# Two-bank score tiles, unscaled k and an ordered start of attention, in a fused attention and expert kernel

## The chip, the cores and the metric

The kernel runs on one core of a Trainium2 chip. The metric is the device time of one execution in microseconds. A core has TensorE (PE, with its weight loads shown apart as PEld), VectorE (DVE), ScalarE (ACT), GpSimd (POOL) and SyncE (SP), which issues the loads here. Matmul results go to eight banks of PSUM, each of 512 float32 numbers for each partition.

## The reference, cut to what matters

Attention with 2 batches, 8 heads, 576 positions and head size 64 is the sum of two softmax attentions: a banded one, and one over positions averaged in fours, whose result is repeated four times. Its output feeds a gated layer (gate, value and output weights), and that an expert layer with eight experts and a normalised routing.

```python
def sm_attn(qq, kk, vv):
    s = scale * np.matmul(qq, kk.transpose(0, 1, 3, 2))      # scale = 1/8
    s = s - np.max(s, axis=-1, keepdims=True)
    a = np.exp(s)
    a = a / (np.sum(a, axis=-1, keepdims=True) + 1e-09)
    return np.matmul(a, vv)
# q_d, k_d, v_d: means over 4 neighbouring positions
out_up = np.repeat(sm_attn(q_d, k_d, v_d), 4, axis=2)
mask = np.abs(pos[:, None] - pos[None, :]) < 4
...                                                          # banded softmax attention
x = out_up + out_local
h = silu(x @ w_gate) * (x @ w_val) @ w_out
out = sum over 8 experts e of P[:, e] * (relu(h @ w1[e]) @ w2[e])   # P from 8 row and column normalisations
```

## The kernel before, in words

Sixteen heads are worked in eight pairs; the two heads of a pair share one k tile and one q tile, whose halves are zeroed so that each head has its own contraction. The banded attention is cut into five windows of 128 positions. `scores(h)` adds the mask by a matmul with an identity (L397, L402), then the window products (L400, L404) and the pooled products of `qd` and `kd` (L406). VectorE takes the maxima (L409 to L411, in fact minima, because k is scaled by -1/8), ScalarE the seven exponentials with their sums (L415 to L420), VectorE the sum and the reciprocal (L423, L424), GpSimd the normalisation (L426, L428). `turn(h)` transposes the result on TensorE (L437 to L441), and ScalarE copies it back (L443 to L445). `combine(pr)` multiplies by v (L457, L465); ScalarE copies the pooled part (L468), VectorE adds it (L474), and the sum is split into two float16 numbers (L169, L170 in `split`).

`pooled(pr)` scales k in place on ScalarE (L373), sums k and q by fours on VectorE (L374, L381) and scales kd (L375). `pooled_v(pr)` does the same for v on GpSimd (L386 to L390). `bank` gives two single-bank tiles out of six for the scores, the transposes or the outputs of a head or pair. Four heads (`AHEAD`) are started before the first is transposed; then each head's transposition is followed by the start of the head four later.

Between the pairs, gate and value weights, which arrive as float64, are converted for use: `conv_gv(f)` loads 1 MB (L186), rebuilds float32 numbers (L198 to L205) and takes their maximum (L220); `prep_gv(f)` finds a power of two (L139 to L142, across partitions with L160 to L162) and splits the weights. `gv_step(0, f, True)` does three early gate steps (matmuls at L177) during pairs 4, 6 and 7. After attention the rest of the gated layer and the experts follow.

The order of the instructions on each engine is made by a planner from the order in the program, priorities, and the costs that it assumes; `issue_after(ins)`, wrapped as `gate(ins)`, forces what stands inside it behind `ins` on the engine of `ins`, without a wait between engines. All loads are in SP's queue. Semaphores follow from the tiles: a reader in a PSUM bank is kept apart from writers in the same bank of a tile.

## Time and profile before

| | us |
|---|---|
| median of 3 runs | 1045.02 |
| lowest and highest run | 1041.98, 1045.06 |
| span of the profiled execution | 1041.1 |
| PE busy | 1013.4 |
| DVE busy | 756.6 |
| ACT busy | 457.7 |
| POOL busy | 81.3 |

The span runs from the first to the last instruction; for the profiled execution the page gives its span alone, and the time of a run also takes in what lies before and after it. Busy time of PE is the time in which a matmul is in work, also a slow one. Attention fills about the first tenth of the span, the gated layer the time to about 330 us, the experts the rest.

### The profile page before, as it was taken

What the parts mean: (1) busy time and instruction counts of PE and PEld (TensorE: products, weight loads), DVE (VectorE), ACT (ScalarE), POOL (GpSimd) and SP (SyncE); (2) the same over time, 40 slices, a digit from 0 to 9 for tenths busy, and PEclk for the clock granted to TensorE, in tenths of its full rate; (3) what the DMA queues carried; (4) which work ended last, traced back from release to release, by engine and by line L of the source; (5) the groups of instructions that cost most, each with busy time, mean ns of one, the idle gap of its engine ahead of it and who ended that gap; (6) DMA issues with size and microseconds to landing.
All of it is one profiled execution on the core that took longest, in us unless ns stands there. A gap on an engine that the chain in (4) does not pass through costs nothing.

```text
span 1041.1 us, 16454 instructions
## 1 busy us (share of the span) xinstructions
PE 1013.4 (97%) x6540; PEld 651.0 (63%) x6541; DVE 756.6 (73%) x1555; ACT 457.7 (44%) x957; POOL 81.3 (8%) x117
## 2 busy tenths in 40 slices
PE   5989899999999999999999999999999999999998
PEld 4978465666577756566655755656565575665644
DVE  6787888965683999797679749749866973974721
ACT  6797576656351746235135215413522631441300
POOL 5664000000000200000000000000000000000000
PEclk8999899999999999999999999999999999999999
DMA  9542242330020022013012110201201211020011
GB/s 213 156 145 68 81 163 92 151 122 1 1 81 2 1 82 95 28 41 122 1 41 82 41 41 16 107 1 41 96 27 41 81 42 41 1 82 1 1 41 51
DMA packets 22459, 65.54 MB, mean 63 GB/s; under 512 B 12080, under 2 KB 12336, under 8 KB 15984
## 3 DMA queue, kind: packets, MB, share of 16 engines
q1 hardware_dynamic: 22384, 64.51, 18.1%
q8 instruction: 51, 0.84, 0.3%
q14 instruction: 24, 0.20, 0.1%
HBM read 62.14 MB, written 2.36 MB: 62 GB/s over the span
## 4 chain that ended last, share of the span: by engine, by line
PE 85%; DVE 7%; DMA 3%; ACT 3%; issue 1%; SPq 0%; ACTq 0%; DVEq 0%
PE y L177 36%; PE p L177 30%; PE gv L177 10%; PE wo L177 4%; DMA rawg<-in_wgv 2%; PE s L400 1%; PE o L465 1%; DMA k<-in_kT 1%; DVE w L170 1%; DMA rawo<-in_wo 1%; PE lgps L593 1%; DVE cvg L204 0%; DVE mxw L146 0%; PE o L457 0%; PE t L437 0%
## 5 line engine op out<-in xcount | busy, mean ns | idle before, releaser
L177 PE MATMUL y<-w,hhl 128*128 128x512 f16 (+1 forms) x1752 | 396.2, 376 | 0.0
L177 PE MATMUL p<-bop,w 128*128 128x320 f16 (+1 forms) x2688 | 354.4, 286 | 0.8 <-DVE u L734 0.7
L177 PEld LDWEIGHTS <-w 128*128 128x128 f16 x2688 | 263.0, 98 | 90.6 <-issue 1.3
L177 PEld LDWEIGHTS <-hhl 128*128 128x128 f16 x1752 | 171.5, 98 | 178.1
L762 ACT ACTIVATE hhl<-h 128x640 f16<-128x640 f32 (+1 forms) x128 | 83.3, 676 | 159.9 <-DVE h L734 159.8
L177 PE MATMUL gv<-xhl,gv 128*128 128x320 f16 (+1 forms) x864 | 144.3, 329 | 2.9 <-ACT gv L169 2.3
L169 ACT ACTIVATE w<-r,s_w 128x256 f16<-128x256 f32 (+1 forms) x96 | 71.2, 783 | 118.0 <-PE y L177 86.3
L177 PEld LDWEIGHTS <-gv 128*128 128x128 f16 x864 | 84.9, 99 | 58.8 <-issue 3.5
L793 DVE SCALAR_TENSOR_TENSOR acc<-y,pe,acc 128x512 f32<-128x512 f32 (+1 forms) x64 | 47.3, 739 | 101.3 <-PE y L177 100.5
L763 DVE SCALAR_TENSOR_TENSOR hhl<-h,hhl 128x640 f16<-128x640 f32 (+1 forms) x128 | 94.4, 752 | 15.3 <-ACT hhl L762 14.0
L734 DVE SCALAR_TENSOR_TENSOR h<-p,u 128x256 f32<-128x256 f32 (+1 forms) x192 | 84.9, 452 | 19.8 <-PE p L177 14.1
L170 DVE SCALAR_TENSOR_TENSOR w<-r,s_w,w 128x256 f16<-128x256 f32 (+1 forms) x96 | 78.0, 831 | 16.8 <-ACT w L169 16.7
L177 PE MATMUL wo<-ahl,wo 128*128 128x320 f16 (+1 forms) x432 | 73.9, 333 | 0.0
L169 ACT ACTIVATE w<-cmb,s_w 128x512 f16<-128x512 f32 x64 | 43.0, 710 | 42.1 <-DVE cmb L274 40.0
L177 PEld LDWEIGHTS <-wo 128*128 128x128 f16 x432 | 43.3, 101 | 28.2
L734 DVE SCALAR_TENSOR_TENSOR u<-p,u 128x320 f32<-128x320 f32 (+1 forms) x128 | 57.2, 447 | 4.1 <-PE p L177 3.2
L156 POOL PARTITION_ALL_REDUCE g_w<-gm_w x16 | 6.3, 392 | 592.7 <-DVE gm_w L152 586.8
L751 ACT ACTIVATE s<-p 128x256 f32<-128x256 f32 (+1 forms) x64 | 25.4, 397 | 56.9 <-PE p L177 56.9
L146 DVE TENSOR_REDUCE mxw<-r 128x1 f32<-128x1024 f32 x32 | 37.4, 1213 | 12.8 <-DMA r<-in_w 12.8
L170 DVE SCALAR_TENSOR_TENSOR w<-cmb,s_w,w 128x512 f16<-128x512 f32 x64 | 45.9, 739 | 0.1
L294 ACT ACTIVATE j<-r 128x1024 f16<-128x1024 f32 x32 | 33.4, 1045 | 24.5 <-DMA r<-in_w 24.5
L170 DVE SCALAR_TENSOR_TENSOR ahl<-act,sc,ahl 128x512 f16<-128x512 f32 (+1 forms) x24 | 19.6, 818 | 17.6 <-ACT ahl L169 17.6
(203 smaller groups left out, 937.9 us busy)
## 6 DMA issues: line engine op xcount, KB each, us to landing
r<-in_w SPq DMA_DIRECT2D x32, 1024.0 KB, 4.8
rawg<-in_wgv SPq DMA_DIRECT2D x12, 1024.0 KB, 4.8
rawo<-in_wo SPq DMA_DIRECT2D x6, 1024.0 KB, 6.3
vz<-in_vw SPq DMA_DIRECT2D x16, 160.0 KB, 3.2
k<-in_kT SPq DMA_DIRECT2D x8, 288.0 KB, 4.3
qz<-in_qT SPq DMA_DIRECT2D x16, 144.0 KB, 5.2
v<-in_vd SPq DMA_DIRECT2D x8, 288.0 KB
out<-acc SPq DMA_DIRECT2D x8, 256.0 KB, 2.0
```

The costliest lines, as they stand in the source:

```text
L146: V.tensor_reduce(o, i, axis=axis, op=ALU.max, apply_absolute_value=True)
L169: return (A.activation(hi, src, AF.Copy, scale=s), V.scalar_tensor_tensor(lo, src, s, hi, op0=ALU.mult, op1=ALU.subtract))
L170: V.scalar_tensor_tensor(lo, src, s, hi, op0=ALU.mult, op1=ALU.subtract))
L177: T.matmul(ps, lhsT=wf(i, k), rhs=xf(j, k), start=n == 0, stop=n == 3 * nk - 1)
L294: A.activation(junk, t[:, 2 * j:2 * j + 2].rearrange("p a n -> p (a n)"), AF.Abs, accum_out=mx[:, 2 * i + j:2 * i + j + 1])
L400: T.matmul(ps[0][:, w * P:(w + 1) * P], lhsT=q[:, j, ws], rhs=k[:, ws], start=False, stop=w == NW - 2)
L465: T.matmul(dst, lhsT=v[:, w, j], rhs=ats[2 * pr + j][:, off:off + hi - lo], start=j == 0, stop=j == 1)
L734: V.scalar_tensor_tensor(o, ps, HSC, u, op0=ALU.mult, op1=ALU.add)
L751: A.activation(s1, p1, AF.Copy, scale=HSC)
L762: ra = A.activation(t[:, 0], h, AF.Relu)
L763: rv = V.scalar_tensor_tensor(t[:, 1], h, 0.0, t[:, 0], op0=ALU.max, op1=ALU.subtract)
L793: V.scalar_tensor_tensor(acc[t][:, ds], ps, p[:, t:t + 1], acc[t][:, ds], op0=ALU.mult, op1=ALU.add)
```

## The change

Scaling: k and kd are no longer scaled on ScalarE. The mask is negative and smaller (128 columns, repeated by the matmul's read), the maxima are maxima, a multiplication by a small constant tile `csc` gives the biases, and the exponentials carry the scale. Score, transpose and output tiles have two banks each and there are three of them; one maximum covers the five windows, and one copy the five transposed windows. The statistics tiles `stm` and `sts` are four in place of two. Order: `pooled` of pairs 2 and later is put behind the reciprocal of the head three before, the first `pooled_v` behind head 1's normalisation; the loads of gate weights 0 and 1 are issued together after four heads, and the conversion of weights 0 is put behind the exponentials of head 5.

```diff
...
     V.tensor_scalar(identb, dist, 0.0, None, op0=ALU.is_equal)
-    maskb = ap.tile([P, 4, P], BF16, tag="maskb", bufs=1, name="maskb")
-    V.tensor_scalar(maskb, dist[:, None, :].to_broadcast([P, 4, P]), FAC * FAC - 0.5, FAR,
-                    op0=ALU.is_ge, op1=ALU.mult)
+    maskb = ap.tile([P, P], BF16, tag="maskb", bufs=1, name="maskb")
+    V.tensor_scalar(maskb, dist, FAC * FAC - 0.5, -FAR, op0=ALU.is_ge, op1=ALU.mult)
...
-    stm = [ap.tile([P, 8], F32, tag=f"stm{i}", bufs=1, name=f"stm{i}") for i in range(2)]
-    sts = [ap.tile([P, 8, 2], F32, tag=f"sts{i}", bufs=1, name=f"sts{i}") for i in range(2)]
+    stm = [ap.tile([P, 8], F32, tag=f"stm{i}", bufs=1, name=f"stm{i}") for i in range(4)]
+    sts = [ap.tile([P, 8, 2], F32, tag=f"sts{i}", bufs=1, name=f"sts{i}") for i in range(4)]
+    csc = ap.tile([P, 8], F32, tag="csc", bufs=1, name="csc")
+    V.memset(csc[:, :5], -SCALE)
+    V.memset(csc[:, 5:], -SCALE / (FAC * FAC))
...
-    for i in range(2):
+    for i in range(4):
...
-    def conv_gv(f, after=None):
-
+    raws = {}
+
+    def load_gv(f):
         with gate(loaded[-1]):
-            raw = load_f64(wgv[f], f"g{f}")
-        with gate(after):
+            raws[f] = load_f64(wgv[f], f"g{f}")
+
+    def conv_gv(f, *after):
+
+        if f not in raws:
+            load_gv(f)
+        raw = raws.pop(f)
+        with ExitStack() as st:
+            for a in after:
+                st.enter_context(gate(a))
...
         def bank(nm):
-            return [psa.tile([P, 512], F32, tag="att", bufs=6, name=f"{nm}_{i}") for i in range(2)]
+            return psa.tile([P, 1024], F32, tag="att", bufs=3, name=nm)
...
             kd[pr] = ap.tile([P, SD], F32, tag="kd", name=f"kd{pr}")
-            A.activation(k, k, AF.Copy, scale=-0.125)
             V.tensor_reduce(kd[pr], k.rearrange("p (s a) -> p s a", a=FAC), axis=AX.X, op=ALU.add)
-            A.activation(kd[pr], kd[pr], AF.Copy, scale=1.0 / (FAC * FAC))
...
             ps = bank(f"s{nm}")
-            T.matmul(ps[0], lhsT=identb, rhs=maskb.rearrange("p u w -> p (u w)"), start=True, stop=False)
-            for w in range(NW - 1):
+            T.matmul(ps[:, :512], lhsT=identb, rhs=maskb[:, None, :].to_broadcast([P, 4, P]), start=True, stop=False)
+            for w in range(NW):
                 ws = slice(WSTART[w], WSTART[w] + P)
-                T.matmul(ps[0][:, w * P:(w + 1) * P], lhsT=q[:, j, ws], rhs=k[:, ws],
-                         start=False, stop=w == NW - 2)
-            T.matmul(ps[1][:, DW:DW + P], lhsT=identb, rhs=maskb[:, 0], start=True, stop=False)
-            ws = slice(WSTART[4], WSTART[4] + P)
-            T.matmul(ps[1][:, DW:DW + P], lhsT=q[:, j, ws], rhs=k[:, ws], start=False, stop=True)
+                if w == 4:
+                    T.matmul(ps[:, w * P:(w + 1) * P], lhsT=identb, rhs=maskb, start=True, stop=False)
+                T.matmul(ps[:, w * P:(w + 1) * P], lhsT=q[:, j, ws], rhs=k[:, ws], start=False, stop=w > 2)
             for t in range(2):
-                T.matmul(ps[1][:HS, t * SD:(t + 1) * SD], lhsT=qd[pr][:, j, t * HS:(t + 1) * HS],
+                T.matmul(ps[:HS, DO + t * SD:DO + (t + 1) * SD], lhsT=qd[pr][:, j, t * HS:(t + 1) * HS],
                          rhs=kd[pr], start=True, stop=True)
-            mx, sm = stm[h % 2], sts[h % 2]
-            V.tensor_reduce(mx[:, :4], ps[0].rearrange("p (u w) -> p u w", u=4), axis=AX.X, op=ALU.min)
-            V.tensor_reduce(mx[:, 4:5], ps[1][:, DW:DW + P], axis=AX.X, op=ALU.min)
-            V.tensor_reduce(mx[:HS, 5:7], ps[1][:HS, :DW].rearrange("p (u w) -> p u w", u=2),
-                            axis=AX.X, op=ALU.min)
+            mx, sm = stm[h % 4], sts[h % 4]
+            V.tensor_reduce(mx[:, :NW], ps[:, :DO].rearrange("p (u w) -> p u w", u=NW), axis=AX.X, op=ALU.max)
+            V.tensor_reduce(mx[:HS, 5:7], ps[:HS, DO:DO + DW].rearrange("p (u w) -> p u w", u=2), axis=AX.X, op=ALU.max)
+            V.tensor_tensor(mx, mx, csc, op=ALU.mult)
             ex = ap.tile([P, NW * P + DW], F32, tag="ex", bufs=6, name=f"ex{nm}")
-            for w in range(4):
-                A.activation(ex[:, w * P:(w + 1) * P], ps[0][:, w * P:(w + 1) * P], AF.Exp, scale=-1.0,
+            for w in range(NW):
+                A.activation(ex[:, w * P:(w + 1) * P], ps[:, w * P:(w + 1) * P], AF.Exp, scale=SCALE,
                              bias=mx[:, w:w + 1], accum_out=sm[:, w, 0:1])
-            A.activation(ex[:, DO - P:DO], ps[1][:, DW:DW + P], AF.Exp, scale=-1.0,
-                         bias=mx[:, 4:5], accum_out=sm[:, 4, 0:1])
             for t in range(2):
-                A.activation(ex[:HS, DO + t * SD:DO + (t + 1) * SD], ps[1][:HS, t * SD:(t + 1) * SD], AF.Exp,
-                             scale=-1.0, bias=mx[:HS, 5 + t:6 + t], accum_out=sm[:HS, 5 + t, 0:1])
+                o = DO + t * SD
+                last = A.activation(ex[:HS, o:o + SD], ps[:HS, o:o + SD], AF.Exp, scale=SCALE / (FAC * FAC),
+                                    bias=mx[:HS, 5 + t:6 + t], accum_out=sm[:HS, 5 + t, 0:1])
+            exp_done[h] = last
             rs = ap.tile([P, 8], F32, tag="rs", name=f"rs{nm}")
             V.tensor_reduce(rs, sm, axis=AX.X, op=ALU.add)
-            V.reciprocal(rs, rs)
+            rs_done[h] = V.reciprocal(rs, rs)
             x = ex[:, :DO].rearrange("p (w k) -> p w k", w=NW)
             G.tensor_tensor(x, x, rs[:, :NW, None].to_broadcast([P, NW, P]), op=ALU.mult)
             x = ex[:HS, DO:].rearrange("p (t k) -> p t k", t=2)
-            G.tensor_tensor(x, x, rs[:HS, 5:7, None].to_broadcast([HS, 2, SD]), op=ALU.mult)
+            norm_done[h] = G.tensor_tensor(x, x, rs[:HS, 5:7, None].to_broadcast([HS, 2, SD]), op=ALU.mult)
             exs[h] = ex
...
-            for w in range(4):
-                T.transpose(pt[0][:, w * P:(w + 1) * P], ex[:, w * P:(w + 1) * P], ident)
-            T.transpose(pt[1][:, DW:DW + P], ex[:, DO - P:DO], ident)
+            for w in range(NW):
+                T.transpose(pt[:, w * P:(w + 1) * P], ex[:, w * P:(w + 1) * P], ident)
             for c in range(2):
                 for t in range(2):
-                    turned[0] = T.transpose(pt[1][:HS, c * SD + t * HS:c * SD + (t + 1) * HS],
+                    turned[0] = T.transpose(pt[:HS, DO + c * SD + t * HS:DO + c * SD + (t + 1) * HS],
                                             ex[:HS, DO + t * SD + c * HS:DO + t * SD + (c + 1) * HS], ident[:HS, :HS])
-            A.copy(at[:, :DO - P], pt[0])
-            A.copy(at[:, DO - P:DO], pt[1][:, DW:DW + P])
-            A.copy(at[:HS, DO:], pt[1][:HS, :DW])
+            A.copy(at[:, :DO], pt[:, :DO])
+            A.copy(at[:HS, DO:], pt[:HS, DO:DO + DW])
...
                 lo, hi = WCUT[w], WCUT[w + 1]
-                dst = ps[0][:, lo:hi] if w < 3 else ps[1][:, lo - base:hi - base]
+                dst = ps[:, lo:hi] if w < 3 else ps[:, 512 + lo - base:512 + hi - base]
...
             if h < NH:
                 if h % 2 == 0:
-                    with tc.issue_after(built[0].ins), tc.issue_after(built[1].ins):
+                    with gate(built[0]), gate(built[1]), gate(rs_done.get(h - 3)):
                         pooled(h // 2)
...
         for h in range(AHEAD):
             start(h)
             if h == 1:
-                pooled_v(0)
+                with gate(norm_done[1]):
+                    pooled_v(0)
                 for i in range(2, NPAIR + 1):
                     load_v4(i)
...
     for n, _ in enumerate(attention()):
         pr, r = divmod(n - AHEAD - 5, 6)
         if n == AHEAD:
-            conv_gv(0)
+            load_gv(0)
+            load_gv(1)
+        if n == AHEAD + 4:
+            conv_gv(0, exp_done[5])
         if r == 0 and pr >= 0:
...
```

## Rows read from the trace of the kernel before

**Rows 1.** The page, busy time, share of the span and instructions of each engine.

```profile
...
PE 1013.4 (97%) x6540; PEld 651.0 (63%) x6541; DVE 756.6 (73%) x1555; ACT 457.7 (44%) x957; POOL 81.3 (8%) x117
```

**Rows 2.** Busy us by stage: PE, PEld, DVE, ACT, POOL; then PEclk, DMA share, GB/s.

```profile
...
16.00:24.06 8.06, 0.00 (x0) 0.00 (x0) 4.02 (x11) 5.82 (x32) 5.57 (x10) 0.78 1.00 238
24.06:28.35 4.29, 4.29 (x24) 4.07 (x25) 1.44 (x5) 1.67 (x6) 4.29 (x6) 0.62 0.57 187
28.35:49.50 21.15, 20.39 (x192) 18.88 (x191) 16.56 (x40) 18.90 (x80) 12.22 (x16) 1.00 0.49 134
49.50:65.66 16.16, 12.69 (x128) 12.14 (x127) 12.65 (x29) 12.78 (x53) 9.12 (x10) 1.00 0.69 201
65.66:108.36 42.70, 42.70 (x332) 35.95 (x332) 34.22 (x86) 34.45 (x126) 23.14 (x25) 1.00 0.24 74
108.36:121.96 13.60, 8.39 (x51) 4.93 (x50) 11.24 (x26) 7.22 (x14) 0.35 (x1) 0.91 0.23 78
121.96:142.50 20.54, 20.54 (x121) 12.35 (x122) 18.16 (x29) 14.44 (x19) 1.62 (x2) 0.89 0.39 153
```

**Rows 3.** Timeline to 30 us: start, duration, engine, line, tiles, idle before and releaser.

```profile
...
11.26 0.37 ACT L415 ACTIVATE ex<-s,stm 128x128 f32<-128x128 f32 x1 [0.28 <-DVE stm L409]
...
11.62 0.36 ACT L415 ACTIVATE ex<-s,stm 128x128 f32<-128x128 f32 x1
...
12.23 0.29 DVE L410 TENSOR_REDUCE stm<-s 128x1 f32<-128x128 f32 x1 [0.25 <-PE s L406]
...
18.71 0.68 ACT L373 ACTIVATE k<-k 128x576 f32<-128x576 f32 x1 [2.25 <-DMA k<-in_kT]
...
19.73 1.35 DVE L381 TENSOR_REDUCE qd<-qz 128x288 f32<-128x1152 f32 x1 [2.33 <-DMA qz<-in_qT]
...
21.37 0.73 POOL L386 TENSOR_TENSOR vt<-v 72x256 f32<-72x256 f32 x1 [2.33 <-DMA v<-in_vd]
21.43 0.19 DVE L424 RECIPROCAL rs<-rs 128x8 f32<-128x8 f32 x1
...
22.75 1.26 POOL L426 TENSOR_TENSOR ex<-ex,rs 128x640 f32<-128x640 f32 x1
...
24.06 1.12 PE L437 MATMUL t<-ident,ex 128*128 128x128 f32 x4 [8.07 <-POOL ex L426]
...
28.27 1.17 ACT L201 ACTIVATE cvg<-rawg 128x1024 f32<-128x1024 f32 x1 [1.97 <-DMA rawg<-in_wgv]
...
28.41 0.60 PE L437 MATMUL t<-ident,ex 128*128 128x128 f32 x4
```

**Rows 4.** Groups by line and shape to 122 us: busy, mean ns, idle before.

```profile
...
L409 DVE TENSOR_REDUCE stm<-s 128x4 f32<-128x512 f32 x16 | 10.8, 677 | 2.6 <-PE s L400 2.5
...
L443 ACT COPY at<-t 128x512 f32<-128x512 f32 x16 | 9.7, 607 | 0.8 <-PE t L437 0.7
...
L373 ACT ACTIVATE k<-k 128x576 f32<-128x576 f32 x8 | 5.6, 694 | 6.3 <-DMA k<-in_kT 6.3
...
L444 ACT COPY at<-t 128x128 f32<-128x128 f32 x16 | 4.8, 301 | 0.0
...
L375 ACT ACTIVATE kd<-kd 128x144 f32<-128x144 f32 x8 | 2.8, 355 | 0.2 <-DVE kd L374 0.2
```

**Rows 5.** Timeline near 55 us.

```profile
...
52.93 1.12 ACT L201 ACTIVATE cvg<-rawg 128x1024 f32<-128x1024 f32 x1 [3.38 <-DMA rawg<-in_wgv]
...
55.69 0.38 PE L162 MATMUL sm_gv<-gr_gv,ones 1*128 1x1 f32 x2 [2.68 <-DVE gr_gv L161]
```

**Rows 6.** Timeline, 77 to 89 us.

```profile
...
77.42 0.38 PE L397 MATMUL s<-maskb,identb 128*128 128x512 bf16 x1
...
79.81 0.66 PE L457 MATMUL o<-at,vdz 72*128 72x144 f32 x4
...
83.46 0.38 ACT L420 ACTIVATE ex<-s,stm 72x144 f32<-72x144 f32 x1
...
88.88 0.80 DVE L474 TENSOR_TENSOR x<-o,avd 128x364 f32<-128x364 f32 x2
```

More of the change, by code (lines that the diff above doesn't have):

```diff
@@ L53 @@
 NSHORT = NPAIR
+SCALE = 0.125
 QDV = (0, 1, 2, 3, 4, 5, 6, 7)
@@ L81, in tile_kernel @@
     V.memset(warm, 0.0)
-    pw = psa.tile([P, 512], F32, tag="att", bufs=6, name="pw")
+    pw = psa.tile([P, 1024], F32, tag="att", bufs=3, name="pw")[:, :512]
     for _ in range(NWARM):
@@ L317, in tile_kernel @@
     v4s = {}
+    exp_done, rs_done, norm_done = {}, {}, {}
     def load_v4(pr):
```

6 lines of the change are left out of this document (3 added, 3 removed).

## The prediction

> **What bounds the kernel now.** I read the page first: PE is busy 97% of the span [rows 1], so a change of attention pays only where PE stands still or runs slowly. Then the busy times by stage [rows 2] show where that is. From 16.00 to 24.06 us PE does nothing; from 24.06 to 28.35 it works at a granted clock of 0.62, most of the time at the lower of its two levels (1.2 against 2.4 GHz), after those 8 us of nothing; from 49.50 to 65.66 it is idle 16.16 - 12.69 = 3.47 us; from 65.66 to 108.36 it is full; from 108.36 to 121.96, the passage into the gate matmuls, it is idle 5.21 us, and the clock is 0.89 in the 20.5 us after. Everything in the change lies before about 110 us.
>
> The timeline of the start [rows 3] says why PE stands for 8.06 us. PE's first transpose (24.06) waits for GpSimd's normalisation of head 0 (22.75), which waits for the reciprocal (21.43), and that sits in VectorE's queue behind the pooled q of pair 3, held 2.33 us until a q load lands (19.73). ScalarE has the same fault: its exponentials stand behind the scaling of pair 3's k, held 2.25 us by that load (18.71), and GpSimd's normalisation stands behind a pooled v (21.37) that waits 2.33 us for its load. Three queues are each blocked at their head by work for a later pair. At 28.27 ScalarE waits 1.97 us more, for the first gate weights, with the exponentials of head 4 behind. The second place [rows 5] is alike: ScalarE waits 3.38 us for the second gate weights (52.93), its later work is late, and PE waits 2.68 us (55.69) for a small result in that line.
>
> **The change, part by part.**
>
> *Front order.* Pooled work of pair 2 now follows the reciprocal of head 1, that of pair 3 the reciprocal of head 3, and the first pooled v the normalisation of head 1; the k scaling is gone from ScalarE. So the three blocks above can't arise; what is late next? I step it through. Head 0's maximum now covers both banks, so it waits for all of its products. Before, the first exponential began at 11.26; the bank-1 maximum alone ran at 12.23, held 0.25 by the pooled products of two heads [rows 3]. With no kd scaling ahead of these I take 12.0, between the two, for the first exponential. One costs 0.36 start to start (11.26 to 11.62), so seven of a head 2.5 us: heads 0 to 3 end at 14.5, 17.0, 19.5 and 22.0. Head 0's row sum, reciprocal (0.19 each) and normalisation (1.26) are done by about 16.3. But three two-bank tiles serve scores, transposes and outputs: scores 0 to 3 take tiles 1, 2, 3 and 1, the first transpose needs tile 2, free after head 1's exponentials at 17.0. So it starts at 17.0 in place of 24.06 (7.1 earlier). Head 4's scores need tile 3, free at 19.5, and head 1's transposes need tile 1, free at 22.0, in place of 28.41: 6.4 earlier. From there the old order of work continues, so I carry **-6.4 us**. The lower bound is -3: PE idles 8.06 in the old row, and ScalarE's four heads back to back may still leave it 5. The upper one is -9.7: all 8.06 and the 0.38 x 4.29 = 1.6 us that the low clock took.
>
> *Gate loads and conversions.* Both first gate weights are loaded together, and the first conversion is put behind head 5's exponentials, so the second load has landed long before it is wanted. The 2.68 us that PE waited go: **-2.7 us**, with 0 (PE then waits for something else) and -3.5 (all idle time of that stage) as bounds. The first conversion isn't late by this: I put head 5's exponentials at about 28, where the conversion ran before (28.27), and PE wants its result only near 55 [rows 5]. On SP the second load now stands ahead of pair 5's loads and the pooled v loads behind them. The DMA engines are full (share 1.00, 238 GB/s) from 16 to 24 us and 0.57 busy after [rows 2]; 1 MB at that rate is 4.4 us. Pair 5 is read from head 10 on, three pairs after head 4, some 35 us at the 11.7 us a pair worked out below, and the old load of pair 3 kept ScalarE only 2.25 us; so the 4.4 us are hidden. Uncovered they would cost 4.4.
>
> *ScalarE's other work.* It loses 8 x (0.694 + 0.355) = 8.4 us for k and kd. The 512- and 128-wide copies of 0.607 and 0.301 become one of 640, by the slope of 0.306 / 384 columns 0.71, which saves 16 x 0.20 = 3.2 us [rows 4]. Of this what counts lies in the front, already in 12.0 and 2.5 per head; from 65.66 PE is full, and ScalarE is busy 34.45 of 42.70 there [rows 2]. I take nothing more; bound -0.8, PE's idle time from 28.35 to 49.50.
>
> *VectorE.* Two maxima (0.677 and about 0.29) become one: the slope of 0.39 / 384 columns makes it 0.81, 0.16 less; the new multiplication of eight columns is priced by the reciprocal of the same size, 0.19 [rows 3, 4]. So +0.03 a head, 0.5 us in all, beside PE (VectorE is busy 0.80 from 65.66 to 108.36): nothing, at worst +0.5. The smaller mask and ten tiny fills end before PE's first score matmul needs them: 0, bounds -0.3 and +0.3. PE's instruction count stays.
>
> *Two-bank tiles.* A score tile is now held to the last of seven exponentials, where its first bank came free after four, three times 0.36 = 1.1 us earlier; a transpose tile about 0.2 longer. I take **+0.5 us** for the pairs in which PE has no gate matmuls to fill with; bounds 0 and +4. The upper bound is weighed against a rule. The bank-1 maximum of 12.23 waited 0.25 for matmuls that write other columns of its bank [rows 3]. The Trainium skill, page "PSUM — Partial Sum Buffer", section on bank collisions, asks exactly this: two engines may not be in one bank and quadrant at once, so readers are guarded by bank and not by address. By that rule each head's only maximum, and so all its exponentials, waits for the pooled products as well; 16 x 0.25 = 4.0 us if each wait were on the path, a sum of -4.6 in place of -8.6. Four heads are started ahead of their transposes, so I count it once, in the 12.0.
>
> **The sum.** -6.4 - 2.7 + 0.5 = -8.6 us on a span of 1041.1: 1032.5. The page gives only this span for the profiled execution; the three runs lie 0.9 to 4.0 us above it, the median 3.9. With 3.9 the forecast is 1036.4, said as 1036. Stages after 122 us move as a whole: their loads are issued as buffers come free, at no fixed time.
>
> **The rivals.**
>
> *More than that (time 1029).* With gate conversions earlier, the passage from 108.36 to 121.96 also shrinks: PE idles 5.21 us there, and the clock of 0.89 costs 0.11 x 20.54 = 2.3 us after it; 7.5 at most, 1036.4 - 7.5 = 1029. For: VectorE is busy 11.24 of 13.60, with conversions in it. Against: the last conversion and its preparation keep their place behind the last pairs' outputs.
>
> *The front gain is smaller (1041).* ScalarE, back to back from 12 to 23 us, paces PE: 3 in place of 6.4, and half of the 2.7 is lost to the next wait: -3 - 1.4 + 0.5 = -3.9. For: PE would still wait for tiles in 17 to 22.
>
> *It doesn't do what it says (1045).* The order is a planner's; if another late load or VectorE's queue holds PE up for the same 8 us, the time stays. VectorE, busy 16.56 of 21.15 and 12.65 of 16.16 in the middle stages, is where that could be. Against: every one of the three blocks is forbidden by name.
>
> *Slower (1049).* The ring of three tiles becomes the bound from head 4 to the end of attention. A pair takes five tiles: two for scores, two for transposes, one for outputs. A score tile's rows run from the mask matmul (77.42) to the last exponential (83.46 + 0.38), 6.4 us; an output tile's from 79.81 to VectorE's addition at 88.88, some 9.8 us [rows 6]; a transpose tile's, 0.6 of PE and 0.71 and a smaller copy of ScalarE, about 2. 12.8 + 9.8 + 4 = 26.6 us over three tiles are 8.9 us a pair. Before, the seven pairs after the first, with three gate steps between, took from 28.41 to about 110, 11.7 each. So the ring decides only if each tile is held 1.7 us longer, as by maxima behind pooled products and additions late on VectorE; at 2.7 us longer a pair takes 8.9 + 5 x 2.7 / 3 = 13.4, which costs 7 x 1.7 = 11.9 and eats the 8.6, +3.3 to +4: 1049. For: one head's tile is now freed at once and not by banks. Against: the 6.4 and 9.8 are whole tiles already, most of it queueing on ScalarE and VectorE.
>
> **How the numbers follow.** 0.3% of 1045 is 3.1 us, about what a measurement can tell from no change: below 1041.9 is faster, above 1048.1 slower. My forecast, 1032 to 1040: 0.58. More: 0.15. Smaller gain, 1040 to 1041.9 for the greater part: 0.10, of which 0.01 falls within 0.3%. No effect: 0.10. Slower: 0.07. So faster 0.58 + 0.15 + 0.09 = 0.82, within 0.3% 0.11, slower 0.07. The range 1029 to 1043 holds the forecast, the smaller gain, half or more of the case with more and a part of no effect; the bounds of the terms (-3 + 0 + 4 is above it, -9.7 - 3.5 = -13.2 is 1032) lie in it but for the first.
>
> **What the profile after should show.** The first transpose at about 17 us, not 24; head 1's at about 22; no row of k or kd scaling; exponentials of heads 0 to 3 without a gap from about 12; no long wait of ScalarE for gate weights; PE idle before 30 us about 5 us less; the end of attention near 100 in place of 108.36; the stretch from there to the end as long as before. It is wrong if the score matmuls of heads 4 to 8 wait for ScalarE's exponentials, if the first exponential comes after 13, if granted clock falls below 1.00 between 28 and 65 us, where a 3.47 us sum of gaps left it at 1.00 [rows 2], or if the passage into the gate matmuls grows.

## The result, and the profile after

The changed kernel takes 1051.57 us, the median of 4 runs (1050.04 to 1055.26), beside 1043.57 for the kernel before in the same session (4 runs, 1041.98 to 1045.06): a ratio of 1.0088, 95% interval 1.0067 to 1.0108. The medians are 8.0 us apart, the ratio puts the difference at 9.2. I had forecast 1036, a gain of 0.8%; it is a loss of 0.9%. The profiled execution took 1055.26, the longest of the four; its span is 1053.5, 12.4 us more than before, so the two traces lie further apart than the medians.

The page of the changed kernel, engines and then granted clock in 40 slices [rows 1]:

```profile
...
PE 1024.0 (97%) x6541; PEld 659.1 (63%) x6541; DVE 753.7 (72%) x1563; ACT 450.3 (43%) x925; POOL 77.0 (7%) x117
...
PEclk9799999999998999999999999999999999999999
```

ScalarE lost 32 instructions and 7.4 us, VectorE and GpSimd are no busier, and PE issues the same matmuls in 10.6 us more: some of its work ran at the lower clock. Busy time by stage of the changed kernel, columns as in [rows 2]; the last output matmul now ends at 121.8 in place of 110.8:

```profile
...
16.00:24.06 8.06, 6.31 (x41) 5.68 (x40) 4.66 (x12) 6.54 (x38) 6.21 (x9) 0.79 0.80 222
24.06:28.35 4.29, 2.66 (x25) 2.69 (x26) 3.25 (x7) 4.29 (x24) 4.29 (x6) 0.76 0.99 375
28.35:49.50 21.15, 17.63 (x127) 16.21 (x125) 12.19 (x32) 12.71 (x50) 11.09 (x16) 0.82 0.41 114
49.50:65.66 16.16, 13.60 (x91) 12.64 (x91) 11.40 (x28) 9.78 (x44) 6.08 (x8) 0.82 0.44 130
65.66:121.80 56.14, 54.36 (x436) 46.10 (x435) 39.68 (x94) 41.38 (x133) 24.34 (x29) 0.99 0.27 84
121.80:132.27 10.47, 5.25 (x24) 2.33 (x23) 8.39 (x23) 4.71 (x9) 0.35 (x1) 0.83 0.04 6
```

From 16 to 24 us the kernel is better than before (6.31 us of PE work in place of none). From 28.35 to 65.66 it is worse: 31.23 us of PE work (218 matmuls) in place of 33.08 (320), and at a granted clock of 0.82 in both stages, where before it was 1.00. The timeline of its start, against [rows 3]:

```profile
...
12.36 0.44 DVE L419 TENSOR_REDUCE stm<-s 72x2 f32<-72x288 f32 x1
...
12.72 0.81 DVE L418 TENSOR_REDUCE stm<-s 128x5 f32<-128x640 f32 x1
...
13.45 0.44 DVE L419 TENSOR_REDUCE stm<-s 72x2 f32<-72x288 f32 x1
13.82 0.15 DVE L420 TENSOR_TENSOR stm<-stm,csc 128x8 f32<-128x8 f32 x1
...
14.07 0.37 ACT L423 ACTIVATE ex<-s,stm 128x128 f32<-128x128 f32 x1 [9.18 <-DVE stm L420]
...
16.68 0.59 PE L408 MATMUL s<-maskb,identb 128*128 128x512 bf16 x1 [3.12 <-ACT ex L427]
...
19.94 0.71 PE L445 MATMUL t<-ident,ex 128*128 128x128 f32 x5
...
25.47 0.70 ACT L450 COPY at<-t 128x640 f32<-128x640 f32 x1
...
25.69 0.74 PE L445 MATMUL t<-ident,ex 128*128 128x128 f32 x5 [2.03 <-POOL ex L436]
```

The first exponential begins at 14.07, not at 12.0: it waits for the multiplication of all eight columns (13.82), and that stands on VectorE behind the pooled maximum of its own head (12.36) and both maxima of head 1 (12.72, 13.45). The fourth head's score matmuls wait 3.12 us for a tile (16.68). The first transpose is at 19.94, 4.1 us earlier than before, but its copy runs at 25.47 only, behind the exponentials of heads 2 and 3: a transpose tile is held 6.5 us, not the 2 that I had put. Head 1's transposes come at 25.69, 2.7 us earlier than before. By the first output matmul nothing of this is left. Times read from the traces of the profiled executions (us; the second to fifth columns are starts, the sixth an end, the seventh the first matmul of the experts):

| kernel | first exponential | first transpose | first output | second output | end of last output | experts begin | span |
|---|---|---|---|---|---|---|---|
| before | 11.3 | 24.1 | 33.4 | 44.2 | 110.8 | 331.4 | 1041.1 |
| changed | 14.1 | 19.9 | 33.5 | 46.6 | 121.8 | 343.5 | 1053.5 |

From the last output on it moves as a whole: to the first long run of gate matmuls 11.2 us before (121.96 in [rows 2]) and 10.5 after, to the experts 220.6 and 221.7, from there to the end 709.7 and 710.0. Of the 12.4 us between the traces 11.0 are there by the end of the last output, and 2.4 by the second output: most of the loss is in attention, behind its first output. Two places of the changed kernel show how, the timeline at the second and the third output:

```profile
...
42.18 0.44 DVE L419 TENSOR_REDUCE stm<-s 72x2 f32<-72x288 f32 x1
...
42.54 1.21 DVE L207 SCALAR_TENSOR_TENSOR cvg<-rawg,cvg 128x1024 uint32<-128x1024 uint32 x1
...
43.67 0.15 DVE L420 TENSOR_TENSOR stm<-stm,csc 128x8 f32<-128x8 f32 x1
...
43.94 0.37 ACT L423 ACTIVATE ex<-s,stm 128x128 f32<-128x128 f32 x1 [3.74 <-DVE stm L420]
...
44.85 1.21 DVE L208 SCALAR_TENSOR_TENSOR cvg<-rawg,cvg 128x1024 uint32<-128x1024 uint32 x1
...
46.02 0.38 ACT L427 ACTIVATE ex<-s,stm 72x144 f32<-72x144 f32 x1
...
46.59 1.12 PE L463 MATMUL o<-at,vdz 72*128 72x144 f32 x4 [3.38 <-issue]
...
57.66 0.44 DVE L419 TENSOR_REDUCE stm<-s 72x2 f32<-72x288 f32 x1
...
58.88 0.67 DVE L205 TENSOR_SCALAR cvg<-cvg 128x1024 f32<-128x1024 f32 x1
...
59.48 0.15 DVE L420 TENSOR_TENSOR stm<-stm,csc 128x8 f32<-128x8 f32 x1
...
59.75 0.37 ACT L423 ACTIVATE ex<-s,stm 128x128 f32<-128x128 f32 x1 [3.10 <-DVE stm L420]
...
61.83 0.38 ACT L427 ACTIVATE ex<-s,stm 72x144 f32<-72x144 f32 x1
...
62.35 1.63 PE L463 MATMUL o<-at,vdz 72*128 72x144 f32 x8 [2.44 <-ACT ex L427]
```

At 46.59 PE has stood 3.38 us, which the profile calls issue; the matmul starts right after the last exponential of head 6 (46.02 + 0.38 = 46.40), whose tile is the third back in the ring. These exponentials waited 3.74 us, to the end of the multiplication (43.67), and that ran on VectorE between two conversions of 1.21 us for the gate weights. At 62.35 it is alike: the conversion (58.88), the multiplication (59.48), the exponentials (59.75, after a wait of 3.10 us), the output (62.35, after 2.44). Not all of these waits belongs to the multiplication. The maxima that it needs were done at 42.62 and 58.10, so it stood 1.05 and 1.4 us behind other work of VectorE (at the start 1.0, from 12.80 to 13.82, both maxima of head 1); the rest is the wait for the maxima themselves. The groups of waits of the changed kernel from 0 to 123 us (us in total, times, longest) have both:

```profile
...
ACT ex L423 <- DVE stm L420: 26.7, 9, 9.2
...
DVE stm L418 <- PE s L415: 9.8, 7, 3.5
...
PE s L408 <- ACT ex L427: 3.8, 2, 3.1
...
PE o L463 <- issue: 3.4, 1, 3.4
PEld o L463 <- ACT ex L427: 3.0, 3, 2.5
...
PE o L463 <- ACT ex L427: 2.4, 1, 2.4
```

In the kernel before no wait of a matmul for an exponential is over 0.3 us in that stretch, and none of an exponential for a maximum over 0.9.

### The profile page after: what moved, and what is told of

Read it like the earlier page. It is cut to its first block, busy times and chain, and to the rows that moved or that the text cites. A ratio compares the mean times of both kernels' runs of the same rounds, so it can differ in the third digit from the quotient of the medians.

```text
span 1053.5 us, 16410 instructions
## 1 busy us (share of the span) xinstructions
PE 1024.0 (97%) x6541; PEld 659.1 (63%) x6541; DVE 753.7 (72%) x1563; ACT 450.3 (43%) x925; POOL 77.0 (7%) x117
## 3 DMA queue, kind: packets, MB, share of 16 engines
HBM read 62.14 MB, written 2.36 MB: 61 GB/s over the span
## 4 chain that ended last, share of the span: by engine, by line
PE 84%; DVE 8%; ACT 4%; issue 2%; DMA 1%; POOL 1%; ACTq 0%; DVEq 0%; POOLq 0%
PE y L180 35%; PE p L180 30%; PE gv L180 8%; PE wo L180 4%; PE o L471 2%; PE s L413 1%; ACT ex L423 1%; DMA rawo<-in_wo 1%; PE lgps L600 1%; PE o L463 1%; DVE w L173 1%; DVE cvg L207 1%; PE t L445 0%; ACT ex L427 0%; DVE cvg L208 0%
## 5 line engine op out<-in xcount | busy, mean ns | idle before, releaser
L306 ACT ACTIVATE j<-r 128x1024 f16<-128x1024 f32 x32 | 33.4, 1045 | 24.5 <-DMA r<-in_w 24.5
L423 ACT ACTIVATE ex<-s,stm 128x128 f32<-128x128 f32 x80 | 28.2, 376 | 29.6 <-DVE stm L420 26.7
```

What stands on the lines that cost most here:

```text
L306: A.activation(junk, t[:, 2 * j:2 * j + 2].rearrange("p a n -> p (a n)"), AF.Abs, accum_out=mx[:, 2 * i + j:2 * i + j + 1])
L423: A.activation(ex[:, w * P:(w + 1) * P], ps[:, w * P:(w + 1) * P], AF.Exp, scale=SCALE, bias=mx[:, w:w + 1], accum_out=sm[:, w, 0:1])
```

## The experiments

Ratios are to the kernel before, run on the same chip in the same session (its medians there: 1043.53, 1041.61, 1042.08, 1042.95 and 1043.11 us for e1 to e4, e5 to e8, e9 to e12, e13 to e16, e17 and e18), with 95% intervals.

**e1: the change with single-bank tiles** (three maxima and three copies again).

```diff
-            return psa.tile([P, 1024], F32, tag="att", bufs=3, name=nm)
+            return [psa.tile([P, 512], F32, tag="att", bufs=6, name=f"{nm}_{i}") for i in range(2)]
```

> The changed kernel with six single-bank tiles again in place of three two-bank tiles: three maxima and three copies a head as before the change, everything else (unscaled k, the multiplication, four statistics tiles, the order) as changed. Theory 1, the ring: tiles held whole to the last exponential or the last copy make PE wait for ScalarE, and the gaps keep PE's granted clock at 0.83; then this run is at 1030 to 1040, granted clock 1.00 from 30 us on, and PE does not wait for exponentials. Theory 2, the order: the instructions forced behind reciprocals and exponentials come too late; then it stays at 1049 to 1053. Theory 3, the longer way from a maximum to its exponentials (one multiplication more): also 1047 to 1053.

**e2: two-bank tiles alone**, on the kernel before, with one window maximum and one copy of 640 columns: the same lines the other way, and

```diff
-            V.tensor_reduce(mx[:, :4], ps[0].rearrange("p (u w) -> p u w", u=4), axis=AX.X, op=ALU.min)
...
+            V.tensor_reduce(mx[:, :NW], ps[:, :DO].rearrange("p (u w) -> p u w", u=NW), axis=AX.X, op=ALU.min)
```

> The kernel before with the two-bank tiles alone: one maximum over five windows, one copy of five windows, k still scaled, the old order. Theory 1 (ring): slower than before by the whole 8 us or more, 1050 to 1058, since the front gain of the order is missing too. Theories 2 and 3: 1042 to 1046, nothing of what they blame is in it.

**e3: order and gate part alone**, on the kernel before (gates of the pooled work, early loads, later conversion, four statistics tiles; k scaled, single banks).

```diff
+                    with gate(built[0]), gate(built[1]), gate(rs_done.get(h - 3)):
                         pooled(h // 2)
...
-            conv_gv(0)
+            load_gv(0)
+            load_gv(1)
+        if n == AHEAD + 4:
+            conv_gv(0, exp_done[5])
```

> The kernel before with the order alone: pooled work on VectorE behind reciprocals, the first pooled v behind head 1's normalisation, both gate loads early, the first conversion behind head 5's exponentials, four statistics tiles. Theory 1 (ring): 1036 to 1043, the first transpose some us earlier than at 24 us. Theory 2 (order): 1049 to 1053. Theory 3: 1036 to 1043 as well.

**e4: k unscaled alone**, on the kernel before (one multiplication, old order, single banks).

```diff
-            A.activation(k, k, AF.Copy, scale=-0.125)
...
+            V.tensor_tensor(mx, mx, csc, op=ALU.mult)
```

> The kernel before with k left unscaled alone: scale in the exponentials, maxima in place of minima, the small mask, the multiplication by a constant tile; six single-bank tiles and the old order. Theory 1 (ring): 1038 to 1044, since ScalarE loses some 8 us of work and one of the three blocks at the start. Theory 2 the same. Theory 3 (longer way to the exponentials): 1046 to 1052.

Measured: e1 1044.39 us, 1.0013 [0.9997, 1.0028]; e2 1049.81, 1.0064 [1.0040, 1.0088]; e3 1040.98, 0.9977 [0.9960, 0.9993]; e4 1049.29, 1.0049 [1.0033, 1.0066]. The parts nearly add up: +0.64 - 0.23 + 0.49 = +0.90% beside +0.88%. That is well inside the intervals, and every edit also lets the planner order other instructions anew, so a run measures its edit and the new order together. None of the three theories stands alone: e1 lies above what the ring theory asked for and below what the others did, and each has a part. The tiles are the largest cost, but k unscaled with its multiplication, which I had priced at 0 and at most +0.5, costs almost as much, and the order brings 2.5 us where I had put 9.1.

**e5: e4 with the multiplication split** (diff), **e9: the multiplication alone**, by ones, with k scaled as before, and **e16: e4 without it**.

```diff
+            V.tensor_tensor(mx[:, :4], mx[:, :4], csc[:, :4], op=ALU.mult)
             V.tensor_reduce(mx[:, 4:5], ps[1][:, DW:DW + P], axis=AX.X, op=ALU.max)
...
-            V.tensor_tensor(mx, mx, csc, op=ALU.mult)
+            V.tensor_tensor(mx[:, 4:], mx[:, 4:], csc[:, 4:], op=ALU.mult)
```

> The kernel before with k unscaled alone (as e4: single-bank tiles, old order), but the multiplication by -scale is split: columns 0 to 3 right behind the maximum of the first bank, columns 4 to 7 behind the other two maxima. In e4 the first exponential began at 16.82 us, 11.92 us of wait on the one multiplication, which stood on VectorE behind the pooled k and q of pair 1; before it began at 11.26. Theory 'the one multiplication ties four window exponentials to the pooled products': the first exponential comes back to 11 to 12 us, the first transpose to 22 us or earlier, and the time falls from 1049.3 to 1044 or less. Rival 'unscaled k is slower for what it does later (exponentials with no scaling work on ScalarE between them, more small operations on VectorE)': the first exponential moves but the time stays at 1047 to 1050.

> The kernel before (k scaled on ScalarE, single-bank tiles, old order) with one multiplication by ones of all eight columns put behind the three maxima, as the changed kernel has it. Theory 'the multiplication, not the unscaled k, is what e4 pays': the first exponential begins near 16 us in place of 11.26 and the time is that of e4 or a little more (the k scaling stays too), ratio 1.005 to 1.008. Rival 'unscaled k itself costs' (other exponentials, another order of the instructions): within 0.2% of before.

> e4 without the multiplication: k unscaled, single banks, old order, but the maxima go straight to the exponentials as their bias (minima are taken, unscaled), so the exponentials here have the wrong bias; its time is that of unscaled k without the new operation. Theory 'all that e4 and e5 cost is the multiplication, as in e9': ratio at most 1.000, perhaps 0.997, since 8.4 us of scaling are gone from ScalarE, and the first exponential at 11 us or earlier. Rival 'unscaled k costs by itself, by another order of the work': 1.002 or more.

Measured: e5 1044.85 us, 1.0025 [1.0011, 1.0038]; e9 1051.54, 1.0091 [1.0076, 1.0106]; e16 1043.11, 1.0007 [0.9992, 1.0022]. The multiplication is the cost: alone it costs more than all of e4 and more than I had expected, and without it the unscaled k costs nothing that can be told (the exponentials of e16 have a wrong bias; only its time is used). It gains nothing either: the 8.4 us of scaling were off the path. What 0.2 us of an instruction can do is in the timeline of e4: it takes its place on VectorE behind the pooled k and q of the next pair, and the first exponential with it.

```profile
...
13.04 0.29 DVE L411 TENSOR_REDUCE stm<-s 128x1 f32<-128x128 f32 x1 [1.12 <-PE s L407]
...
14.83 1.34 DVE L382 TENSOR_REDUCE qd<-qz 128x288 f32<-128x1152 f32 x1
...
16.09 0.70 DVE L414 TENSOR_TENSOR stm<-stm,csc 128x8 f32<-128x8 f32 x2
...
16.82 0.37 ACT L417 ACTIVATE ex<-s,stm 128x128 f32<-128x128 f32 x1 [11.92 <-DVE stm L414]
```

This late start isn't where e4 loses its time: its first transpose (22.85 us, before 24.06) and its first three outputs (31.7, 43.2 and 55.0, before 33.4, 44.2 and 56.1) come earlier than before. It falls behind from the fourth output on (68.3 against 67.6), and its last output ends at 114.2 against 110.8. Where the multiplication costs time is seen in e9, at the third output:

```profile
...
54.21 0.44 DVE L413 TENSOR_REDUCE stm<-s 72x2 f32<-72x288 f32 x1
...
57.62 0.15 DVE L415 TENSOR_TENSOR stm<-stm,csc 128x8 f32<-128x8 f32 x1
...
57.89 0.37 ACT L418 ACTIVATE ex<-s,stm 128x128 f32<-128x128 f32 x1 [1.76 <-DVE stm L415]
...
59.45 0.85 PE L460 MATMUL o<-at,vdz 72*128 72x144 f32 x2 [1.92 <-ACT ex L418]
```

The last maximum ends at 54.65, the multiplication of 0.15 us comes 3.0 us later, behind other work of VectorE; the exponentials wait 1.76 us for it, and PE 1.92 for the exponentials. The granted clock is 0.79 from 49.50 to 65.66 us (1.00 before), and the last output ends at 118.1.

In e5 the first exponential is back at 11.80, in e16 at 10.67 us; e9 has it at 18.26. By the ratios e5 keeps about half of e4's cost, and it misses its forecast of 1044 or less; its first transpose comes at 23.37, later than e4's, so the half that it wins isn't an earlier front. Which waits of the two small instructions a head make up its cost stays open. The Trainium skill, page "Perfetto Trace Analysis", section on optimizing Scalar and DVE operations, says that where these engines are not saturated but hold up others, breaking instructions up may let work finish sooner. e5 against e4 agrees (1.0025 against 1.0049), but two cases below don't: e8, which splits the multiplication of the change, is no faster than the change, and e10 with three maxima and three copies is slower than e2 with one of each.

**e10: two-bank tiles with the three maxima and three copies of before**, so the same instructions in other tiles; **e8: the changed kernel with the multiplication split** (columns 0 to 4 behind the window maximum):

```diff
+            V.tensor_tensor(mx[:, :NW], mx[:, :NW], csc[:, :NW], op=ALU.mult)
```

> The kernel before with two-bank tiles alone, all its three maxima and three copies kept (e2 had one window maximum and one copy of 640 columns). Theory 'the ring of three tiles costs, whatever reads them': ratio 1.005 to 1.009, as e2, last output near 115 us. Rival 'the wider maximum or the wider copy comes too late in e2': within 0.2% of before, last output near 111.

> The changed kernel with only the multiplication split: columns 0 to 4 right behind the window maximum, columns 5 to 7 behind the pooled maximum; tiles of two banks stay. Theory 'ring of three tiles': a tile is still held to its last exponential, so the time stays near 1051, at best 1048 by a first exponential some 0.5 to 1 us earlier, and the last output still ends near 120 us. Rival 'the tie is most of the loss also with two-bank tiles': 1045 or less and the last output near 114.

Measured: e10 1054.75 us, 1.0123 [1.0108, 1.0138]; e8 1051.85, 1.0094 [1.0064, 1.0123], no better than the change. In two-bank tiles the split didn't even bring the first exponential forward (14.42 us): the window maximum ends at 12.80, but the multiplication behind it runs at 14.17 only, behind the head's own pooled maximum (12.71) and both maxima of head 1 (13.08, 13.81). So e8 doesn't test what an earlier first exponential would bring. e10 is above the 1.005 to 1.009 that I had expected. The single maximum and copy are no cost, they repair half of what the tiles do (e2 against e10). e10's waits of PE for exponentials to 115 us (us in total, times, longest):

```profile
...
PEld o L453 <- ACT ex L417: 4.9, 3, 2.9
PE o L453 <- ACT ex L417: 4.4, 3, 2.8
```

and the longest of them in its timeline:

```profile
...
71.33 2.29 PE L453 MATMUL o<-at,vdz 72*128 72x144 f32 x8 [2.76 <-ACT ex L417]
```

It's the fourth output, and PE begins it only after the last exponential of head 10 (70.80 + 0.38 = 71.18). Before, with single banks, the same output begins while that exponential is still to come:

```profile
...
67.59 0.66 PE L457 MATMUL o<-at,vdz 72*128 72x144 f32 x4
...
67.89 0.48 ACT L420 ACTIVATE ex<-s,stm 72x144 f32<-72x144 f32 x1
```

And the kernel before at its third output:

```profile
...
58.03 0.60 PE L437 MATMUL t<-ident,ex 128*128 128x128 f32 x4
...
58.47 0.66 PE L457 MATMUL o<-at,vdz 72*128 72x144 f32 x4
...
59.83 0.27 PE L438 MATMUL t<-ident,ex 128*128 128x128 f32 x1
```

Four transposes of a head run at 58.03, an output's matmuls at 58.47, and the fifth transpose, which goes to the second bank, at 59.83. I read these rows so: with single banks PE uses the half of a pair of banks that is free and comes back for the other, and a tile of two banks is had whole or not at all. The order is the planner's, and no run shows this reading alone.

**e11: single banks, but released late; e12: its control.** Before the first matmul of each use, one of one column that reads what the last reader of the use three back wrote (in e12 a constant). Both kernels also have four `sts` tiles.

```diff
+    def wait_free(ps):
+        if len(uses) > 2:
+            x = uses[-3].bitcast(BF16)[:, 1:2]
+            T.matmul(ps, lhsT=x, rhs=x, start=True, stop=True)
```

> The kernel before with its single-bank tiles, but the first matmul of every use of a pair of banks (scores, transposes, outputs) is preceded by a one-column bf16 matmul that reads what the last reader of the use three back wrote (the last exponential's sum, the last copy, the last addition), as if the two banks were one tile. Theory 'a tile of two banks costs because its first bank is no longer given back early': against its control (e12) slower by 4 to 7 us, last output near 115 us, PE rows that wait for the last exponential. Rival 'the cost of two-bank tiles comes from the order that the planner makes of the matmuls, not from the late release': within 2 us of the control.

> Control of e11: the same one-column matmuls, but reading a constant tile, so that they wait for nothing. Some 40 of them at under 0.1 us, most in PE's idle time: within 0.3% of before (0 to 3 us slower).

Measured: e11 1052.01 us, 1.0091 [1.0075, 1.0108]; e12 1048.67, 1.0057 [1.0039, 1.0075]. The control missed what I expected, 0 to 3 us, and is told in part by its own rows: 37 such matmuls are recorded with 0.164 us each, and the next matmul begins 0.09 to 0.10 us after most of them and 0.32 after seven, some 5 us in all. That most of the 5.9 us it lost are this is an estimate from these rows. Against it the late release costs 0.0034 x 1042 = 3.5 us, with an interval of about 1 to 6 us, as the two intervals touch. The last output ends at 121.7 in place of 115.3 us, but e11's profiled execution is its longest, so the traces show too much. The 3.5 is a little under what the ring theory said, and the 2 us of its rival are not ruled out. So the release accounts for some 3.5 us of the 6.7 to 12.8 of e2 and e10 at best estimate; that the rest is the lost interleaving and the order built around it is argued from the rows above, not shown by a run.

**e6 and e7: the second gate weight loaded where it was before**, in e3, and in e1 with the multiplication split.

```diff
             load_gv(0)
-            load_gv(1)
```

> The kernel before with the new order alone (as e3), but the second gate weight is loaded where the kernel before loaded it, not together with the first. In e3 the loads of k took 7.91 and 10.63 us beside two gate loads of 1 MB, ScalarE waited 3.17 and 2.24 us for k at 25.35 and 37.74 us, and head 3's transposes began at 39.2. Theory 'the second gate load of 1 MB, which I priced as hidden, takes bandwidth from k and q of pairs 3 and 4 and gives back part of the front gain': those waits fall under 1 us, the second output begins at 42 us or earlier in place of 44.4, and the time falls from 1041.0 to 1038 or 1039. Rival 'the load was hidden, something else in pair 1 gives the gain back': 1041 plus or minus 1, and the late wait for the second gate weights (3.38 us before) comes back, so perhaps 1043.

> The changed kernel without its three suspected costs: single-bank tiles with three maxima and three copies, the multiplication split as in e5, and the second gate weight loaded where it was before; k unscaled and the order of the front as in the change. If the costs are the tiles, the tie and the load, and add up: e1 1044.4, less some 4 for the tie, less 0 to 2 for the load: 1038 to 1040, below the kernel before by 4 to 6. First transpose at 17 us. If unscaled k costs by itself, 1043 to 1045 as e1.

**e13: the front order alone** (the first part of e3's diff)**; e14: the gate part alone** (the second)**; e15: e3 again.**

> The kernel before with the front order alone: pooled work of a pair behind the reciprocal three heads back, the first pooled v behind the normalisation of head 1, four statistics tiles; gate loads and conversions as before. My prediction's term is -6.4 us. If the front's gain holds, 1036 to 1038 for a kernel before of 1042 to 1043 (ratio 0.994); if it is given back by pair 1 and the passage into the gate matmuls, as the last output of e3 (110.5 against 110.8) suggests, ratio 0.998 to 1.000, with the first transpose near 18 us and the last output at 109 to 111.

> The kernel before with the gate part alone: both first gate weights loaded together, the first conversion behind the exponentials of head 5. My prediction's term is -2.7 us. If it holds, ratio 0.997, no wait of ScalarE for the second gate weights. If the two loads of 1 MB take the DMA from k and q (e3: loads of 7.9 and 10.6 us on the chain of waits), 0 to +3 us: ratio 1.000 to 1.003.

> The kernel of e3 again (order and gate part, k scaled, single banks), in five rounds. e3 gave 0.9977 [0.9960, 0.9993]; I expect 0.996 to 0.999, so faster than the kernel before by 1 to 4 us, and faster than the changed kernel by 9 to 12.

**e17: e3 with the scaling of k held back**, behind the exponentials of the head before; **e18: e17 with the second load as in e6.**

```diff
-                    with gate(built[0]), gate(built[1]), gate(rs_done.get(h - 3)):
+                    with gate(built[0]), gate(built[1]), gate(rs_done.get(h - 3)), gate(exp_done.get(h - 1) if h > 2 else None):
```

> The kernel of e3 and e15 (order and gate part, k scaled, single banks) with the scaling of k of pairs 2 and up also put behind the exponentials of the head before. In e3 ScalarE waited 3.17 us (25.35) and 2.24 us (37.74) for loads of k with exponentials behind them. Theory 'these blocked exponentials give the front's gain back': the waits for k fall under 1 us each, the second output begins at 41 to 42 us in place of 44.4, the time falls to 1038 or 1039, ratio 0.995 to 0.997. Rival 'the loads themselves are late, so the score matmuls wait instead': the ratio stays at 0.998 to 0.999.

> e17 with the second gate weight loaded where the kernel before loads it (as e6). If load and blocked scaling add up as causes, the lowest of all: ratio 0.994 to 0.996. If it goes as in e6 (0.9991, no gain from the later load), 0.998 to 1.000.

Measured: e6 1041.26 us, 0.9991 [0.9973, 1.0009]; e7 1042.30, 1.0008 [0.9992, 1.0024]; e13 1040.95, 0.9987 [0.9968, 1.0006]; e14 1042.04, 0.9994 [0.9981, 1.0006]; e15 1041.15, 0.9988 [0.9975, 1.0002]; e17 1040.97, 0.9982 [0.9965, 0.9999]; e18 1042.63, 0.9995 [0.9983, 1.0007]. The load theory falls for the time. Of e3's two waits for k one is gone in e6 (2.24 us at 37.74) and one is left (2.36 us at 24.65, where I had put it under 1). e6 has its second output at 38.1 us, 6.3 before e3, and its last output ends 3.2 earlier, but the experts begin only 1.2 earlier and the time is no lower. Beside e15, the same program as e3, the second output is 3.7 earlier and the experts begin 3.3 later: such differences between two traces show little. The same of the scaling of k: e17 has its second output at 39.2 and no long wait for k, and e3's ratio, not the 0.995 to 0.997 that I expected; e18 went as e6 did. e7 missed its 1038 to 1040 and can't be told from the kernel before. In e14 ScalarE's wait for the second gate weights is gone, and PE's waits for the small result behind it fall from 4.3 us to 1.6, but PE waits 3.0 us for the gate weights themselves (2.3 before). What the front gives at each point (profiled executions, us less than the kernel before):

| kernel | first transpose | first output | second output | end of last output | experts begin | span |
|---|---|---|---|---|---|---|
| e13 | 5.6 | 6.6 | 3.7 | 3.1 | 3.2 | 2.1 |
| e17 | 5.3 | 5.7 | 5.0 | 3.0 | 2.5 | 2.6 |
| e3 | 6.2 | 5.4 | -0.2 | 0.3 | 1.2 | 1.1 |
| e15 | 6.4 | 6.2 | 2.4 | 2.9 | 5.7 | 5.5 |

In the rows of e13, e17 and e3 the gain shrinks by the end of the stage. e15 is e3's program in an execution that is the lowest of its twelve: two executions of one program differ by 2.6 us at the second output and 4.4 in the span, so smaller differences between rows show nothing.

In e13 the timeline shows where ScalarE stands next, for the k of the next pair and for the gate weights:

```profile
...
24.23 0.69 ACT L374 ACTIVATE k<-k 128x576 f32<-128x576 f32 x1 [1.88 <-DMA k<-in_kT]
...
29.60 1.12 ACT L201 ACTIVATE cvg<-rawg 128x1024 f32<-128x1024 f32 x1 [2.20 <-DMA rawg<-in_wgv]
```

Work that is ready earlier meets loads that are not. A part of what is lost after the second output is the clock: in e13 it is 0.92 from 28.35 to 49.50 us and 0.89 from 49.50 to 65.66, where before it was 1.00, which on 19.2 and 14.2 us of PE work makes 0.08 x 19.2 + 0.11 x 14.2 = 3 us, an estimate from these rows. The rest stays open. The order with its gate part (e3 and its repeat e15, and e17 with k held back) is the only version here with an interval below 1: 0.9977, 0.9988 and 0.9982, two of the three, so 1 to 2.5 us faster than the kernel before, and some 11 than the changed one.

## Why the prediction was wrong

**Front order, -6.4.** The mechanism was right: in e13 the first output comes 6.6 us earlier. Two of its assumptions were not. In the changed kernel the first exponential came at 14.07 and not at 12.0, since I let it wait for the pooled products but not for the new multiplication behind them and the maxima of head 1 that stand ahead of it; the first transpose, forecast at 17.0, came at 19.94. And "From there the old order of work continues" didn't hold: the order alone keeps 1.4 us at the end (e13, interval 3.3 faster to 0.6 slower), with the gate part 2.4 and 1.2 (e3, e15).

**Gate loads, -2.7.** Mis-sized: e14 gives -0.6 us (interval -2.0 to +0.6). The wait that I priced went, and PE waits 3.0 us for the gate weights (2.3 before), near what the bound of 0 had as its condition. That the second load is hidden, as I had put it, is right of the time; in pair 1 one wait for k of e3 goes without it (e6).

**ScalarE's other work, 0.** Right: e16 shows that the scaling of k was off the path.

**VectorE, nothing, at worst +0.5.** The step that failed first. The sizes were right and the price was not, as the groups by line and shape of the changed kernel to 122 us show [rows 4]:

```profile
...
L418 DVE TENSOR_REDUCE stm<-s 128x5 f32<-128x640 f32 x16 | 13.1, 818 | 9.9 <-PE s L415 9.8
...
L450 ACT COPY at<-t 128x640 f32<-128x640 f32 x16 | 11.1, 694 | 3.7 <-PE t L448 3.7
...
L420 DVE TENSOR_TENSOR stm<-stm,csc 128x8 f32<-128x8 f32 x16 | 3.3, 210 | 0.1
```

The multiplication takes 0.210 us (0.19 forecast), the maximum 0.818 (0.81), the copy 0.694 (0.71); but e9 shows 9.5 us for the one new instruction. I priced it by its duration; what it costs is its place in VectorE's queue, between the maxima and all the exponentials of a head. In the change it stood 1.0, 1.05 and 1.4 us behind other work at the three places above, in e9 3.0 us at 57.62. The 26.7 us in nine waits that end with it aren't all its own: the first, 9.2 us, holds the loads and the scores as well.

**Two-bank tiles, +0.5, at most +4.** The step that failed most: 6.7 us (e2), or (1.0088 - 1.0013) x 1043.5 = 7.8 from e1 to the change. It is 12.8 with three maxima and copies (e10). My rival "slower" was this mechanism: it set 13.4 us a pair and 1049 us, at a chance of 0.07. The outputs of the changed kernel stand at 33.5 and, five pairs on, at 103.0 us, 13.9 a pair (before 33.4 and 94.1, 12.1); with the tiles alone it is 12.9 (e2) and 13.4 (e10). That its 1049 lies near the measured 1051.6 is in part luck: it charged the ring 11.9 us and left 8.6 of gains, where the runs give the tiles 6.7 to 7.8, the multiplication 5.1 and the order a gain of 2.4. It "decides only if each tile is held 1.7 us longer", and the hold of a transpose tile was the size that I had wrong: "about 2" counts its own matmuls and copies, not the queue of their reader. The transpose tile of head 0 was held 6.5 us in the change, as its copy queues on ScalarE behind the exponentials of other heads. The trace of before had it already, from 24.06 [rows 3] to the end of its last copy, 7.2 us:

```profile
...
30.84 0.43 ACT L445 COPY at<-t 72x288 f32<-72x288 f32 x1
```

The rule of the Trainium skill that the prediction weighed, page "PSUM — Partial Sum Buffer", bank collisions, may have a part in it: the window maximum has 9.8 us of waits that end with pooled products into its bank, seven of 1.4 each in the mean, where I had taken 0.25 [rows 3]. What guarding by bank adds to such a wait is at most the time of these products, 0.65 to 1.2 us each: the longest wait, 3.49 us to 32.91, ends with products that began at 31.71. The rest of that wait lies before them. And its page "Perfetto Trace Analysis", section on the optimization strategy, says that a gap that comes again and again on the engine that should be full can mean too little PSUM for the next tile: the gaps at 16.68 and 62.35, which end with exponentials, agree, and the one at 46.59 begins its matmul 0.2 us after such an end.

**The clock.** I named a granted clock below 1.00 between 28 and 65 us as a sign of error; it was 0.82 there. Within it the stretches differ: 0.58 from 28.35 to 34.0, 1.00 from there to 46.6, 0.53 and 0.55 to 54.0 behind the gap of 3.38 us at 46.59, about 1.00 to 64.0, and 0.73 from 64.0 to 70.0 behind the gap of 2.44. So two low stretches follow the gaps, and the first comes before either. The two stages by run (28.35 to 49.50, then 49.50 to 65.66): 1.00 and 0.79 in e1 and in e9, 0.98 and 1.00 in e2 and in e10, 1.00 and 1.00 before. So the low clock of the second stage goes with the multiplication and not with the tiles. That gaps lowered it is argued; no run shows it alone. Two more of my signs came true, the first exponential after 13 (14.07) and score matmuls that wait for exponentials (3.12 us at 16.68); the passage into the gate matmuls did not grow.

The sum as measured: order -2.4, multiplication with k unscaled +5.1, tiles +6.7, together +9.4 us; the change costs 9.2. Each of these has an interval of about 2 us to either side, so the sum shows that no large part is missing, and no more.

## What to carry to other kernels

Price a new small instruction by the queue it stands in and by what waits behind it, not by its duration: 0.2 us of VectorE between a maximum and its exponentials cost 5 to 9.5 us here. Before merging banks into one tile, work out how long each tile is held with every reader's queue counted, and compare with the uses it needs: a coarser ring may also take from the matmul engine the choice of which half to work on. A gain at the front of a full kernel is worth only what the next load, the next tile and the next queue leave of it; look for it at the last point of the stage before it is booked.

## What the hardware showed that was not expected

A matmul of one column on 72 partitions (bf16) is recorded with 0.164 us, as all 37 in e12 are, and the next matmul began 0.09 to 0.32 us after it: tiny matmuls put in for their waits are not free. Runs of one kernel differ with their mean granted clock: of 28 runs of the kernel before in one session the lowest (1040.68 us) has 0.992 and the highest (1048.22) 0.985, so a profile that happens to be the lowest of its kernel, as in e4 (span 1042.8, median run 1049.29), hides a part of the cost. And beside the two gate loads of 1 MB the loads of k, 288 KB each, took 7.91 and 10.63 us on the chain of waits of e3 (start, us, what). With one gate load less (e6) the first still took 7.3 us and the second at most 6.3, so only the second shows what the second gate load does, and the time of e6 is no lower:

```profile
...
17.42 7.91 DMA k<-in_kT
...
27.09 10.63 DMA k<-in_kT
```
